# Features of q on both column halves of TensorE: an attention and Fourier-mix kernel, before and after

## The chip, the cores and the metric

The kernel runs on one core of a Trainium2 chip. The metric is the device time of one execution in microseconds (us). The engines are TensorE (PE in the profile, its weight loads PEld), VectorE (DVE), ScalarE (ACT), GpSimd (POOL) and SyncE (SP), which issues the transfers between HBM and on-chip memory.

## What is computed

The inputs q, k, v have 4 batches, 4 heads, 1088 rows and 32 dimensions in float32. S1 and S2 are 8 x 32.

```
phi(x)  = outer product of S1 x and S2 x, 64 features for each row
kv, z   = sum over rows of phi(k) v  and of phi(k)
attn    = (phi(q) kv) / (phi(q) z + 1e-6)            # per head, 32 values a row
x       = the 4 heads beside one another              # 4 x 1088 x 128
u       = x + real(FFT over the 1088 rows and the 128 columns of x)
out     = u + relu(layernorm(u) w_ch1) w_ch2          # w_ch1 128 x 512
```

## The kernel before

One batch at a time is cut into named steps, each on one engine. A text, ORDER, lists all steps of all batches; the kernel emits them in that order, and each engine runs its own in that sequence and waits for what it needs. BANK gives the first of eight PSUM banks for each use, ENGINE the engine where a step can run on several. In the names, the first digit is the batch b.

- **Loads** (ld_q, ld_k, ld_v, ld_w1, ld_w2 on SP, ld_s on ACT). A partition of q holds 34 successive rows: four heads lie on four blocks of 32 partitions. Work on q is done in two windows w of 16 rows and 256 positions a pair; the rows left over are handled by qt_T, qt_f, qt_a, qt_p.
- **Start** (c_... steps, t_... tables of sines, s_t and s_use, which make sa and sb, the operands of S1 and S2, 32 x 64 per head). Dummy matmuls such as 7@0 keep TensorE busy; the number is how many, then the bank.
- **k side**: kT (transposition, L299), kpr (projection, L289), kab (copy from PSUM), kp (products, L76, 16 of them, POOL or DVE), vc and vl (copies of v), kv and kvt (sums over rows, L337), kvz (L343: copies to the operand t_kvz, for each batch two pairs of heads, each head in its own diagonal block of 64 x 33).
- **q side**: qT (L376, transposition of one window, output with a step of 8 elements), qf (qfeat, L383), qa (copy of one factor from PSUM, ACT), qp (L393, product of the two factors, 128 x 1024, DVE). In qfeat, one instruction takes sa or sb of head h (32 rows of the array, 32h on) against 256 columns of qT. Its output goes to 64 partitions of PSUM: heads 0 and 2 to the left column half of the array, heads 1 and 3 to the right. A window takes 4 heads x 2 halves of the columns x 2 factors = 16 instructions.
- **pnd** (L433): products with t_kvz as the moving operand, 66 columns, weights 128 x 64 from qp: two heads on the two partition halves. 32 instructions a batch, and pnt has 4 for the rows left over. Each float32 matmul leaves two records in the trace. Then den and x (L439 to L444: division, result in bf16).
- **Fourier mix and MLP**: fo and eo (folds by symmetry, POOL or DVE), sC and sS (L461, L465), z and zr (copies), mix (L487, L494; it adds x by a matmul with a permutation), and for each mixer g bn (statistics, L515), sd, rc, un (normalization, L532), tr, ut (transposition), ph (L546), rl (relu, L561 on ACT, L563 on DVE), po (L568), fin (copy to the output tile), out (store). There are ten mixers; eight have 512 columns, mixers 4 and 9 have 128.

The order of the work around the change is thus wholly the text ORDER with the banks: a use of a bank waits until the use before it has been read. A group of features takes four banks: q0.0, q0.1 and q1.1 take 0 to 3, q1.0 takes 1 to 4.

Of the kernel before, what the change touches and what calls it, by code (L numbers as in the profile page):

```python
# [52 lines left out]
def program(nc, T, x, bank):  # L53
# [187 lines left out]
    def c_rev(e):  # L241

        nc.gpsimd.memset(T("rev")[:], 0.0)
        nc.gpsimd.affine_select(out=T("rev")[:], in_=T("rev")[:], compare_op=ALU.not_equal, fill=1.0, base=-127,
                                pattern=[[1, 128]], channel_multiplier=1)
    add("c_rev", "POOL", "", "rev", c_rev)
# [126 lines left out]
    def qT(b, w):  # L373

        out = [[1, 8], [-256, 2], [8, 32]] if w == 0 else [[1, 8], [256, 2], [8, 32]]
        nc.vector.transpose(view(T(f"qT{b % 2}"), (256, 512)[w], out), view(T(f"q_in{b}"), (1, 18)[w] * D, [[1, 16 * D]]))  # L376


    def qfeat(b, w):
        for i in range(2):  # L380
            for h in range(H):
                for f, src in enumerate(("sa", "sb")):
                    nc.tensor.matmul(  # L383
                        ps(f"q{b}.{w}", 512 * (2 * (h // 2) + i) + 256 * f, [[1, 256]], 64 * (h % 2), 64),
                        view(T(src), 0, [[1, F]], 32 * h, 32), view(T(f"qT{b % 2}"), 512 * w + 256 * i, [[1, 256]], 32 * h, 32),
                        start=True, stop=True, tile_position=(32 * h, 64 * (h % 2)), skip_group_check=True)
# [36 lines left out]
    def pnd(b, tiles):  # L423

        for s in tiles:
            for pr in range(2):
                for h in range(2):
                    if s < 8:
                        w = s // 2 % 2
                        q = view(T(f"qp{(2 * b + w) % 3}"), 512 * pr + 256 * (s % 2) + 128 * (s // 4 ^ w) + 64 * h, [[1, 64]])  # L430
                    else:
                        q = view(T("qtp"), 256 * pr + 64 * b, [[1, 64]])
                    nc.tensor.matmul(ps(f"nd{b}", 512 * (s // 3) + 132 * (s % 3) + 66 * pr, [[1, 66]], 64 * h, 64), q,  # L433
                                     view(T("kvz"), 2 * KP * b + KP * pr, [[1, 66]]), start=True, stop=True,
                                     tile_position=(0, 64 * h), skip_group_check=True)
# [47 lines left out]
    def mix(b, half):  # L483
        u = f"u{b}.{half}"
        for w in range(2):
            s = (6, 2)[half] if w else 4 * half
            nc.tensor.matmul(ps(u, 256 * w, [[1, 256]]), T("rev" if w else "idb")[:],  # L487
                             view(T(f"x{b}"), 128 * (s + 1 - w), [[256 * w - 128, 2], [1, 128]]),
                             start=(w == 0), stop=False, skip_group_check=True)
# [218 lines left out]
c_wz c_iota ld_q0.0 c_bias c_rows d_turn c_last d_ph d_pm c_kvz c_v12 c_mask c_eye16 t_turn2 c_vt c_v11 ld_s c_v10  # L708
c_idb c_cen t_ph2 c_rev 7@0 s_t qT0.0 s_use 5@1 qf0.0 d_trig t_sin2 t_turn1 ld_k0.0 t_pm2 t_cos2 t_turn0 kT0.0 1@4
kpr0 t_mC qa0.0 ld_k1.0 kab0 ld_v0 kp0.0 qT0.1 kT1.0 kp0.3 kp0.1 kt_pr0 3@6 kpr1 qp0.0 kt_a0 t_ph1 ld_q1.0 qt_T1 qt_T0  # L710
qf0.1 vl0 ld_v1 ld_k2.0 vc0.0 vc0.1 qa0.1 kt_p0 qt_f0 kv0.0 kab1 kvt0 kv0.3 t_ph0 qT1.1 qp0.1 kv0.1 ld_q2.0 ld_w1
ld_v2 ld_v3 ld_q3.1 kt_pr1 ld_k3.1 ld_k3.0 ld_q3.0 kp0.2 ld_w2 kp1.1 kv0.2 t_pm1 qt_a0 vc1.0 kp1.0 kp1.3 kp1.2 qf1.1
vl1 t_pm0 kt_a1 qt_p0 kT2.0 kt_p1 qT1.0 kvz0 t_sin0 qa1.1 t_mS vc1.1 pnd0.0 pnt0 qp1.1 kpr2 pnd0.1 qT2.0 qT2.1 den0 x0
kv1.0 kab2 qf1.0 kv1.2 kv1.1 kvt1 kv1.3 kt_pr2 w1c t_sin1 qa1.0 qp1.0 qt_T2 kt_a2 vl2 kt_p2 kT3.0 kvz1 kp2.1 kp2.2 w1b
t_cos0 kp2.0 qf2.0 fo0.0 fo0.1 vc2.1 kp2.3 eo0.0 qa2.0 vl3 vc2.0 t_cos1 pnd1.0 pnt1 kpr3.0 pnd1.1 qT3.1 kT3.1 kpr3.1
kab3 qt_T3 qp2.0 qf2.1 den1 x1 qa2.1 kv2.2 kv2.3 kv2.1 qt_f1 vc3.1 kvt2 kv2.0 kp3.1 eo0.1 fo1.0 qp2.1 qt_a1 kvz2 qf3.1
vc3.0 kt_pr3 fo1.1 qt_p1 pnd2.0 qa3.1 kt_a3 kt_p3 pnt2 kvt3 eo1.1 t_mP t_mN pnd2.1 qp3.1 sS0 w2b qT3.0 den2 zS0 x2
kp3.0 eo1.0 kp3.3 sC0 kv3.1 sC1 zC1 zC0 mix0 qf3.0 kp3.2 zrC0 fo2.1 fo2.0 eo2.0 bn0 sd0 rc0 un0 zrC1 sS1 qa3.0 zS1
zrS0 kv3.2 kv3.0 kv3.3 tr0 qp3.0 mix2 ut0 ph0.1 kvz3 zrS1 ph0.0 mix1 rl0.1 rl0.0 pnd3.0 pnt3 eo2.1 bn2 sS2 bn1 sd1 rc1
sd2 rc2 pnd3.1 un1 zS2 un2 tr2 ut2 tr1 ut1 po0 den3 x3 fin0 ph1.0 ph1.1 rl1.1 mix3 rl1.0 zrS2 fo3.0 mix4 ph2.1 rl2.1  # L720
ph2.0 po1 sC2 bn3 bn4 fo3.1 eo3.1 rl2.0 po2 sd3 rc3 eo3.0 un3 tr3 sd4 rc4 ut3 zC2 zrC2 sC3 fin1 ph3.1 mix5 un4 fin2
zC3 rl3.1 ph3.0 tr4 bn5 ut4 sd5 rl3.0 sS3 out0 out2 rc5 un5 mix6 zS3 ph4.0 tr5 ut5 bn6 out1 rl4.0 po3 sd6 rc6 un6 fin3
# [3 lines left out]
"""
BANK = dict(w.split("=") for w in """
st=0 w1=6 k0=4 kt0=5 kv0=5 k1=4 kt1=4 kv1=0 k2=4 kt2=5 kv2=7 k3=7 kt3=7 kv3=7 qt0=6 qt1=4 q0.0=0 q0.1=0 nd0=5 z00=2
z10=0 u0.0=2 t0=0 h0.0=6 h0.1=3 u0.1=0 t1=7 h1.0=6 h1.1=3 q1.0=1 q1.1=0 nd1=4 z01=0 z11=0 u1.0=1 t2=6 h2.0=3 h2.1=6
u1.1=2 t3=3 h3.0=6 h3.1=3 u0.2=5 t4=1 h4.0=6 q2.0=0 q2.1=0 nd2=4 z02=6 z12=6 u2.0=0 t5=7 h5.0=6 h5.1=3 u2.1=1 t6=2  # L730
h6.0=3 h6.1=6 q3.0=3 q3.1=0 nd3=3 z03=6 z13=3 u3.0=2 t7=7 h7.0=0 h7.1=3 u3.1=5 t8=3 h8.0=0 h8.1=3 u1.2=6 t9=7 h9.0=7
# [3 lines left out]
d_turn=DVE t_pm2=ACT t_mC=ACT kt_a0=DVE vl0=DVE vc0.0=ACT vc0.1=ACT t_pm1=ACT vl1=ACT t_pm0=ACT kt_a1=DVE t_mS=ACT  # L735
vc1.1=ACT vl2=ACT fo0.0=POOL fo0.1=POOL eo0.0=POOL vl3=ACT vc2.0=ACT vc3.1=ACT eo0.1=POOL fo1.0=POOL kt_a3=DVE w2b=ACT
eo1.0=POOL zC1=DVE fo2.1=POOL fo2.0=POOL eo2.0=POOL zrS0=ACT ut0=DVE zrS1=ACT zS2=DVE un2=ACT rl1.0=DVE fo3.0=POOL
fo3.1=POOL eo3.1=POOL rl2.0=DVE eo3.0=POOL ut3=DVE fin2=DVE ut4=DVE rl4.0=DVE fin4=DVE ut6=DVE fin6=DVE ut7=DVE
ut9=DVE rl7.1=DVE fin9=DVE fin8=DVE
# [32 lines left out]
```

## Time and profile before

| | |
|---|---|
| median of three runs | 91.48 us (90.75 to 91.81) |
| the profiled execution | 91.52 us, its span 89.7 us |
| granted TensorE clock | 0.999 |
| busy: PE, DVE, ACT, POOL | 78.6, 64.2, 56.7, 46.3 us |
| transfers | 9.65 MB, 7.22 MB read |
| a store of 128 KB, of 64 KB, from issue to landing | 2.4 us, 1.7 us |

The span goes from the first to the last instruction; about 1.8 us of the execution lie outside it. A line of a group reads: line, engine, operation, output <- input, shapes, count, then busy time and the mean length of one in ns, then the idle time before it with what ended it. The chain is followed backwards from the last instruction; its pieces are shown in order of time with their start and length.

### The profile page before, as it was taken

The page shows a single profiled execution, that of the slowest core. Times are in us where ns is not written, and L with a number is a line of the kernel's source. Part 1 is how long each engine was busy: PE and PEld are TensorE (multiplying, and loading weights), DVE is VectorE, ACT ScalarE, POOL GpSimd, SP SyncE. Part 2 cuts the span into 40 slices and gives each one's busy share as a digit, 9 for nine tenths or more (in the row PEclk, how much of TensorE's full clock was granted, in tenths as well). Part 3 has the DMA queues.
Part 4 walks back from the last instruction along what each step waited for, and adds up shares of the span by engine and source line. Part 5 has one row for each costly group of instructions (what it writes and reads, how often), then busy time and mean ns, then how long its engine had stood idle before and what let it go on. Part 6 is the DMA issues. An engine that isn't in the chain of part 4 may idle for free.

```text
span 89.7 us, 3227 instructions
## 1 busy us (share of the span) xinstructions
PE 78.6 (88%) x1379; PEld 58.9 (66%) x1385; DVE 64.2 (72%) x130; ACT 56.7 (63%) x101; POOL 46.3 (52%) x73
## 2 busy tenths in 40 slices
PE   4949999899499999999989999998999999889600
PEld 1126688779478589787947787796685777756500
DVE  3879999697884947481998856779866888596300
ACT  2373795649504758482949298856767798899400
POOL 7688099895479980899915950024973020000000
PEclk9999999999999999999999999999999999999999
DMA  2999999993000000000000000000400615007362
GB/s 41 380 359 388 389 421 393 390 358 108 9 7 7 4 0 7 0 11 0 0 7 0 0 0 7 0 0 7 117 0 0 187 54 146 0 0 186 84 167 67
DMA packets 6142, 9.65 MB, mean 108 GB/s; under 512 B 624, under 2 KB 3952, under 8 KB 6128
## 3 DMA queue, kind: packets, MB, share of 16 engines
q1 hardware_dynamic: 6048, 9.44, 31.1%
q8 instruction: 11, 0.18, 0.8%
q14 instruction: 3, 0.02, 0.1%
q10 hardware_dynamic: 80, 0.01, 0.1%
HBM read 7.22 MB, written 2.23 MB: 105 GB/s over the span
## 4 chain that ended last, share of the span: by engine, by line
PE 70%; ACT 8%; DVE 6%; DMA 5%; issue 4%; ACTq 1%; DVEq 0%
PE ps L383 17%; PE ps L337 11%; PE ps L433 8%; PE ps L568 6%; PE ps L546 5%; DMA t_s<-in_S_dram 5%; PE ps L289 4%; PE ps L461 4%; PE ps L494 3%; PE ps L699 2%; ACT t_v_in__96 L561 2%; ACT t_v_in__98 L561 2%; PE ps L487 2%; PE ps L465 2%; PE ps L538 2%
## 5 line engine op out<-in xcount | busy, mean ns | idle before, releaser
L69 ACT COPY t_qa__127<-ps 128x1024 f32<-128x1024 f32 x4 | 4.1, 1013 | 6.7 <-PE ps L383 6.7
L69 ACT COPY t_qa__128<-ps 128x1024 f32<-128x1024 f32 x4 | 4.0, 1012 | 4.8 <-PE ps L383 4.8
L699 PE MATMUL ps<-t_wz 128*128 128x512 bf16 x15 | 5.4, 496 | 1.3 <-DVE t_eps L125 1.2
L383 PE MATMUL ps<-t_qT__114,t_sa 32*64 32x256 f32 x64 | 5.4, 395 | 0.0
L383 PE MATMUL ps<-t_qT__115,t_sa 32*64 32x256 f32 x64 | 5.4, 395 | 0.0
L383 PE MATMUL ps<-t_qT__114,t_sb 32*64 32x256 f32 x64 | 5.2, 374 | 0.0
L383 PE MATMUL ps<-t_qT__115,t_sb 32*64 32x256 f32 x64 | 5.2, 374 | 0.0
L73 POOL COPY t_zr__148<-t_z__144 128x546 bf16<-128x546 bf16 x2 | 1.3, 640 | 7.0 <-DVE t_z__144 L71 6.6
L433 PE MATMUL ps<-t_kvz,t_qp__130 128*64 128x66 f32 x96 | 3.7, 225 | 1.3 <-issue 1.3
L546 PEld LDWEIGHTS <-t_w1b 128*128 128x128 bf16 x40 | 3.2, 97 | 2.4 <-issue 1.2
L433 PEld LDWEIGHTS ps<-t_kvz,t_qp__130 128*64 128x64 f32 x96 | 3.2, 138 | 1.6 <-issue 1.5
L561 ACT ACTIVATE t_v_in__96<-ps 128x1024 bf16<-128x1024 f32 x4 | 3.9, 1020 | 0.4 <-PE ps L494 0.4
L561 ACT ACTIVATE t_v_in__97<-ps 128x1024 bf16<-128x1024 f32 (+1 forms) x4 | 3.6, 920 | 0.7 <-PE ps L546 0.7
L699 PEld LDWEIGHTS <-t_wz 128*128 128x128 bf16 x16 | 1.6, 114 | 3.5 <-issue 1.8
L76 POOL TENSOR_TENSOR t_kp__119<-t_ab__117 128x512 f32<-128x512 f32 x2 | 2.1, 1068 | 2.9 <-ACT t_ab__117 L69 2.9
L383 PEld LDWEIGHTS ps<-t_qT__114,t_sa 32*64 32x64 f32 x64 | 2.3, 130 | 1.9 <-ACT t_kvz L69 0.8
L76 POOL TENSOR_TENSOR t_eo__140<-t_e__138 128x512 bf16<-128x512 bf16 x3 | 3.5, 1152 | 0.1
L76 POOL TENSOR_TENSOR t_eo__141<-t_e__139 128x512 bf16<-128x512 bf16 x3 | 3.4, 1153 | 0.1
L433 PE MATMUL ps<-t_kvz,t_qp__129 128*64 128x66 f32 x96 | 3.4, 224 | 0.0
L433 PEld LDWEIGHTS ps<-t_kvz,t_qp__129 128*64 128x64 f32 x96 | 3.0, 138 | 0.6 <-issue 0.4
L546 PE MATMUL ps<-t_unT__161,t_w1b 128*128 128x512 bf16 (+1 forms) x14 | 3.4, 333 | 0.1
L561 ACT ACTIVATE t_v_in__98<-ps 128x1024 bf16<-128x1024 f32 x3 | 3.0, 1021 | 0.7 <-POOL t_e__139 L76 0.6
(320 smaller groups left out, 267.0 us busy)
## 6 DMA issues: line engine op xcount, KB each, us to landing
out_dram<-t_k_in__93 SPq DMA_DIRECT2D x6, 128.0 KB, 2.4
out_dram<-t_k_in__95 SPq DMA_DIRECT2D x6, 128.0 KB, 2.4
t_q_in__100<-in_q_dram SPq DMA_DIRECT2D x1, 544.0 KB, 3.8
...
t_q_in__101<-in_q_dram SPq DMA_DIRECT2D x1, 544.0 KB, 8.4
...
```

Source lines behind the costliest of these rows:

```text
L69: nc.scalar.copy(out, in_)
L76: (nc.vector if e == "DVE" else nc.gpsimd).tensor_tensor(out=out, in0=in0, in1=in1, op=op)
L289: nc.tensor.matmul(ps(f"k{b}", 64 * t, [[1, 64]], 64 * h, 64), view(T(f"kT{b % 2}"), 64 * (2 * t + h), [[1, 64]]), T("sblk")[:], start=Tru ...
L337: nc.tensor.matmul(ps(f"kv{b}", 33 * (h // 2), [[1, 33]], 64 * (h % 2), 64), w, v, start=(b, h % 2) not in begun, stop=True, tile_position ...
L383: nc.tensor.matmul(ps(f"q{b}.{w}", 512 * (2 * (h // 2) + i) + 256 * f, [[1, 256]], 64 * (h % 2), 64), view(T(src), 0, [[1, F]], 32 * h, 32 ...
L433: nc.tensor.matmul(ps(f"nd{b}", 512 * (s // 3) + 132 * (s % 3) + 66 * pr, [[1, 66]], 64 * h, 64), q, view(T("kvz"), 2 * KP * b + KP * pr, ...
L461: nc.tensor.matmul(ps(f"z{trig}{b}", 512 * c, [[1, NK]]), T(f"eo{b % 2}")[:, trig, c, t, :], T("tab")[:, t, trig, NK * c:NK * c + NK], sta ...
L494: nc.tensor.matmul(ps(u, 256 * w + 128 * t, [[1, 128]]), zcol(b, trig, half, w, t), m, start=False, stop=True, skip_group_check=True)
L546: nc.tensor.matmul(ps(use, 128 * n * i, [[1, 128 * n]]), T("w1b")[:, 128 * c:128 * c + 128], T(f"unT{g % 3}")[:, 0:128 * n], start=True, s ...
L561: nc.scalar.activation(out=out, in_=in_, func=ACT.Relu)
L568: nc.tensor.matmul(ps(u, 128 * t, [[1, 128]]), ht_view(g, 512 * c + 128 * t, [[1, 128]]), T("w2b")[:, c, :], start=False, stop=True, skip_ ...
L699: nc.tensor.matmul(made["ps"][:, at, :], made["wz"][:, 0:128], made["wz"][:], start=True, stop=True)
```

## The change

- **qfeat**: each head is now handled by two instructions per factor that differ in the column half: half v takes the first or the second 16 of each 32 successive columns of qT (one half of the head's rows), both from the same 32 partitions. Their results go to partitions 64v on of one bank per head. The loops run over h, then v, then the factor.
- **qT**: the output of the transposition is contiguous in runs of 32.
- **kvz**: since the two partition halves of the features now belong to one head, each head's block of 64 x 33 is written twice, to both diagonal blocks: four copies a batch for two, the tile and its clearing memset (c_kvz) twice as large.
- **pnd**: 16 blocks (window, tile, head) of two instructions for 8 tiles x 2 pairs x 2; the counts stay the same. The values of x lie in another order, so fold, mix and the row numbers in c_rows follow, and a second permutation (c_fwd) is made for the mix.
- **ORDER, BANK, ENGINE** are all new. The first four groups of features, q0.0, q1.0, q0.1 and q1.1, all take banks 0 to 3. On VectorE instead of GpSimd are kp0.3, kp1.3, kp3.0 and t_turn1; qa3.1 goes from ScalarE to VectorE; many others change too.

```
-        out = [[1, 8], [-256, 2], [8, 32]] if w == 0 else [[1, 8], [256, 2], [8, 32]]
+        out = [[32, 8], [512 * w - 256, 2], [1, 32]]
...
     def qfeat(b, w):
-        for i in range(2):
-            for h in range(H):
+        for h in range(H):
+            for v in range(2):
                 for f, src in enumerate(("sa", "sb")):
                     nc.tensor.matmul(
-                        ps(f"q{b}.{w}", 512 * (2 * (h // 2) + i) + 256 * f, [[1, 256]], 64 * (h % 2), 64),
-                        view(T(src), 0, [[1, F]], 32 * h, 32), view(T(f"qT{b % 2}"), 512 * w + 256 * i, [[1, 256]], 32 * h, 32),
-                        start=True, stop=True, tile_position=(32 * h, 64 * (h % 2)), skip_group_check=True)
+                        ps(f"q{b}.{w}", 512 * h + 256 * f, [[1, 256]], 64 * v, 64), view(T(src), 0, [[1, F]], 32 * h, 32),
+                        view(T(f"qT{b % 2}"), 512 * w + 16 * v, [[256, 2], [32, 8], [1, 16]], 32 * h, 32),
+                        start=True, stop=True, tile_position=(32 * h, 64 * v), skip_group_check=True)
...
     def kvz(b, e):
         for h in range(2):
-            copy(e, view(T("kvz"), 2 * KP * b + 33 * h, [[KP, 2], [1, 33]], 64 * h, 64),
-                 ps(f"kv{b}", 0, [[33, 2], [1, 33]], 64 * h, 64))
+            for v in range(2):
+                copy(e, view(T("kvz"), KP * (H * b + h) + 33 * v, [[2 * KP, 2], [1, 33]], 64 * v, 64),
+                     ps(f"kv{b}", 0, [[33, 2], [1, 33]], 64 * h, 64))
...
+    def pnd(b, blocks):
+        for i in blocks:
+            w, t, hd = i // 8, i // 4 % 2, i % 4
+            for h in range(2):
+                if i < 16:
+                    q = view(T(f"qp{(2 * b + w) % 3}"), 256 * hd + 128 * t + 64 * h, [[1, 64]])
+                    z = view(T("kvz"), KP * (H * b + hd), [[1, 66]])
+                else:
+                    q = view(T("qtp"), 256 * (i - 16) + 64 * b, [[1, 64]])
+                    z = view(T("kvz"), KP * (H * b + 2 * (i - 16)), [[KP + 33, 2], [1, 33]])
+                nc.tensor.matmul(ps(f"nd{b}", 512 * (i // 6) + 66 * (i % 6), [[1, 66]], 64 * h, 64), q, z,
+                                 start=True, stop=True, tile_position=(0, 64 * h), skip_group_check=True)
...
     def fold(b, e, c):
-        tt(e, T(f"e1{b % 2}")[:, c], T(f"x{b}")[:, 0:4, :], T(f"x{b}")[:, 4:8, :], (ALU.add, ALU.subtract)[c])
+        tt(e, T(f"e1{b % 2}")[:, c], view(T(f"x{b}"), 0, [[512 + 32, 2], [64, 8], [1, 32]]),
+           view(T(f"x{b}"), 32, [[512 - 32, 2], [64, 8], [1, 32]]), (ALU.add, ALU.subtract)[c])
...
-    "vt": ([128, 2 * B, VP], FP32), "kvz": ([128, B, 2, KP], FP32),
+    "vt": ([128, 2 * B, VP], FP32), "kvz": ([128, B, H, KP], FP32),
```

The new ORDER, with stretches of it left out:

```
c_wz c_iota ld_q0.0 c_bias c_rows c_eye16 c_mask c_idb t_turn1 ld_s c_last ld_k1.0 ld_k0.0 c_fwd c_rev c_vt c_cen 7@0
s_t t_turn0 c_kvz t_ph1 t_turn2 c_v11 t_pm1 t_cos1 qT0.0 qt_T0 s_use 3@1 qf0.0 qT0.1 kT1.0 ld_q1.0 qa0.0 t_ph0 t_pm0
kT0.0 ld_v0 4@4 kpr1 kab1 t_sin0 t_sin1 kp1.0 t_cos0 c_v12 c_v10 vc0.1 qt_T1 2@5 kpr0 ld_w1 qt_f0 kab0 kp0.2 ld_v1 vl1
kt_pr0 kt_pr1 qp0.0 qT1.0 kp0.1 ld_k2.0 qt_a0 kt_a0 qt_p0 kp0.0 qf1.0 vc1.0 kp0.3 kt_p0 vl0 kt_a1 t_ph2 vc0.0 qa1.0
w1c w1b t_pm2 vc1.1 kv0.3 kvt0 kv0.2 qp1.0 ld_k3.0 ld_k3.1 ld_q3.0 ld_q2.0 ld_w2 ld_v3 kv0.1 qf0.1 kv0.0 t_mP kT2.0
kp1.3 qT1.1 kpr2 kp1.1 kt_p1 kv1.3 kvt1 kv1.0 qa0.1 qp0.1 kab2 t_sin2 ld_v2 ld_q3.1 kv1.1 kvz0 qf1.1 pnd0.0 t_mS qa1.1
kp1.2 kv1.2 kT3.1 pnd0.1 pnt0 qT2.0 qT2.1 kT3.0 kvz1 kp2.3 qp1.1 kt_pr2 t_cos2 kt_a2 vc2.0 vc2.1 vl2 pnt1 qt_T2 den0
kt_p2 x0 qt_T3 pnd1.1 pnd1.0 qf2.1 den1 kpr3.0 kpr3.1 x1 qa2.1 qp2.1 kvt2 kp2.1 kv2.1 qt_f1 fo0.1 kp2.2 kp2.0 vc3.1
...
kv3.2 den2 x2 fo2.1 kt_pr3 zC1 d_ph qf3.1 zC0 kt_a3 d_pm d_trig kt_p3 qa3.1 qp3.1 sS1 zS1 kvt3 kv3.1 mix0 kvz3 mix2
bn0 bn2 sd0 rc0 un0 zrS1 sd2 pnd3.0 zrC1 fo2.0 eo2.0 eo2.1 pnt3 sC2 zrS0 zrC0 pnd3.1 zC2 rc2 tr0 ut0 sS2 zS2 mix1
...
out6 out5 tr8 out7 ut8 mix4 bn4 mix9 rl3.0 rl3.1 sd4 ph8.1 ph8.0 bn9 rc4 rl8.1 po3 sd9 un4 tr4 rl8.0 po8 fin8 fin3 rc9
out3 ut4 un9 out8 tr9 ph4.0 ut9 ph9.0 rl4.0 po4 fin4 out4 rl9.0 po9 fin9 out9
```

and the old one's end:

```
ph9.0 ph7.0 rl9.0 po8 po9 fin9 out9 fin8 out8 rl7.0 po7 fin7 out7
```

More of the change, by code (lines that the diff above doesn't have):

```diff
@@ L239, in program, with order @@
     add("c_idb", "POOL", "", "idb", lambda e: eye(T("idb")[:], 128))
[L241 to L246, printed above, removed]
+    def order(n, sign, base):
+        t = T(n)[:]
+        nc.gpsimd.memset(t, 0.0)
+        nc.gpsimd.affine_select(out=t, in_=t, compare_op=ALU.not_equal, fill=1.0, base=base,
+                                pattern=[[sign, 16], [16 * sign, 8]], channel_multiplier=1)
+    add("c_fwd", "POOL", "", "fwd", lambda e: order("fwd", -1, 0))
+    add("c_rev", "POOL", "", "rev", lambda e: order("rev", 1, -127))
     def c_mask(e):
@@ L421, in program @@
         add(f"qt_p{i}", "DVE", f"pqt:{i} qta:{i}", f"qtp:{i}", lambda e, i=i: qt_p(i), f"qt{i}:2")
[L423 to L435, printed above, removed]
+    def pnd(b, blocks):
[10 more added lines that the diff above has]
+                                 start=True, stop=True, tile_position=(0, 64 * h), skip_group_check=True)
     def den(b):
@@ L485, in mix @@
         for w in range(2):
-            s = (6, 2)[half] if w else 4 * half
-            nc.tensor.matmul(ps(u, 256 * w, [[1, 256]]), T("rev" if w else "idb")[:],
-                             view(T(f"x{b}"), 128 * (s + 1 - w), [[256 * w - 128, 2], [1, 128]]),
+            nc.tensor.matmul(ps(u, 256 * w, [[1, 256]]), T("rev" if w else "fwd")[:],
+                             view(T(f"x{b}"), 512 * w + 256 * (1 - w) + 32 * half, [[512 * w - 256, 2], [64, 4], [1, 32]]),
                              start=(w == 0), stop=False, skip_group_check=True)
@@ L621, in program @@
             add(f"pnd{b}.{pr}", "PE", f"qp:{2 * b + pr} kvz:{b}", f"pnd:{b}/{pr}",
-                lambda e, b=b, pr=pr: pnd(b, [4 * v + 2 * pr + t for v in range(2) for t in range(2)]), f"nd{b}:3")
-        add(f"pnt{b}", "PE", f"qtp:{b // 2} kvz:{b}", f"pnd:{b}/2", lambda e, b=b: pnd(b, (8,)), f"nd{b}:3")
+                lambda e, b=b, pr=pr: pnd(b, range(8 * pr, 8 * pr + 8)), f"nd{b}:3")
+        add(f"pnt{b}", "PE", f"qtp:{b // 2} kvz:{b}", f"pnd:{b}/2", lambda e, b=b: pnd(b, (16, 17)), f"nd{b}:3")
         add(f"den{b}", "DVE", f"pnd:{b}", f"den:{b}", lambda e, b=b: den(b), f"nd{b}:3")
@@ L634, in program @@
         for half in range(2):
-            mixer(b, half, g, (f"zC:{b} zS:{b}", f"zrC:{b} zrS:{b}")[half] + f" x:{b} idb rev cd sd")
+            mixer(b, half, g, (f"zC:{b} zS:{b}", f"zrC:{b} zrS:{b}")[half] + f" x:{b} fwd rev cd sd")
             g += 1
@@ L707 @@
 ORDER = """
[L708 to L722, printed above, removed]
@@ new lines @@
+kt_p2 x0 qt_T3 pnd1.1 pnd1.0 qf2.1 den1 kpr3.0 kpr3.1 x1 qa2.1 qp2.1 kvt2 kp2.1 kv2.1 qt_f1 fo0.1 kp2.2 kp2.0 vc3.1
+vc3.0 fo0.0 fo1.0 qf2.0 kv2.0 kv2.2 kv2.3 qT3.1 t_mN t_mC w2b qT3.0 kab3 qt_a1 qa2.0 qt_p1 eo0.1 sS0 kp3.3 fo1.1 vl3
+qp2.0 kp3.2 eo0.0 eo1.1 kp3.1 d_turn kvz2 kv3.3 zS0 qf3.0 eo1.0 kp3.0 pnd2.1 qa3.0 pnt2 pnd2.0 kv3.0 qp3.0 sC1 sC0
+kv3.2 den2 x2 fo2.1 kt_pr3 zC1 d_ph qf3.1 zC0 kt_a3 d_pm d_trig kt_p3 qa3.1 qp3.1 sS1 zS1 kvt3 kv3.1 mix0 kvz3 mix2
+bn0 bn2 sd0 rc0 un0 zrS1 sd2 pnd3.0 zrC1 fo2.0 eo2.0 eo2.1 pnt3 sC2 zrS0 zrC0 pnd3.1 zC2 rc2 tr0 ut0 sS2 zS2 mix1
@@ new lines @@
+ph0.1 un2 rl0.1 den3 x3 fo3.1 bn1 tr2 ut2 ph0.0 rl0.0 sd1 fo3.0 rc1 eo3.0 mix5 ph2.1 rl2.1 ph2.0 rl2.0 po0 sC3 fin0
+eo3.1 sS3 un1 bn5 zC3 zrS2 tr1 ut1 zS3 sd5 po2 ph1.1 rl1.1 zrC2 ph1.0 rc5 fin2 un5 rl1.0 mix6 bn6 sd6 mix7 zrS3 zrC3
+bn7 tr5 rc6 un6 ut5 sd7 po1 fin1 ph5.0 rc7 rl5.0 un7 tr6 ph5.1 ut6 ph6.0 out0 out2 rl5.1 out1 rl6.0 mix3 bn3 ph6.1
+rl6.1 tr7 ut7 po5 ph7.1 fin5 sd3 rl7.1 ph7.0 po6 rl7.0 rc3 un3 fin6 mix8 bn8 tr3 po7 ut3 sd8 rc8 un8 fin7 ph3.0 ph3.1
+out6 out5 tr8 out7 ut8 mix4 bn4 mix9 rl3.0 rl3.1 sd4 ph8.1 ph8.0 bn9 rc4 rl8.1 po3 sd9 un4 tr4 rl8.0 po8 fin8 fin3 rc9
@@ L726 @@
+out3 ut4 un9 out8 tr9 ph4.0 ut9 ph9.0 rl4.0 po4 fin4 out4 rl9.0 po9 fin9 out9
 """
 BANK = dict(w.split("=") for w in """
[L728 to L731, printed above, removed]
+st=0 w1=6 k0=5 kt0=4 kv0=4 k1=4 kt1=5 kv1=7 k2=6 kt2=7 kv2=0 k3=7 kt3=0 kv3=7 qt0=6 qt1=1 q0.0=0 q0.1=0 nd0=4 z00=5
@@ L732 @@
+z10=1 u0.0=0 t0=4 h0.0=2 h0.1=6 u0.1=4 t1=0 h1.0=2 h1.1=6 q1.0=0 q1.1=0 nd1=0 z01=3 z11=5 u1.0=5 t2=1 h2.0=2 h2.1=6
+u1.1=2 t3=0 h3.0=3 h3.1=6 u0.2=5 t4=3 h4.0=2 q2.0=3 q2.1=3 nd2=0 z02=6 z12=6 u2.0=1 t5=6 h5.0=6 h5.1=3 u2.1=0 t6=2
+h6.0=6 h6.1=3 q3.0=3 q3.1=1 nd3=1 z03=6 z13=2 u3.0=5 t7=6 h7.0=3 h7.1=6 u3.1=1 t8=0 h8.0=6 h8.1=3 u1.2=0 t9=3 h9.0=3
 """.split())
@@ L734 @@
 ENGINE = dict(w.split("=") for w in """
[L735 to L739, printed above, removed]
+t_turn1=DVE t_pm1=ACT t_pm0=ACT qt_a0=DVE kt_a0=DVE kp0.3=DVE vl0=ACT kt_a1=DVE vc0.0=ACT t_pm2=ACT vc1.1=ACT
+kp1.3=DVE t_mS=ACT vc2.0=ACT vc2.1=ACT vl2=ACT fo0.0=POOL fo1.0=POOL t_mC=ACT w2b=ACT eo0.1=POOL fo1.1=POOL eo0.0=POOL
+eo1.1=POOL kp3.0=DVE kt_a3=DVE qa3.1=DVE zrS1=ACT fo2.0=POOL eo2.0=POOL eo2.1=POOL fo3.1=POOL ut2=DVE rl0.0=DVE
+fo3.0=POOL rl2.0=DVE eo3.1=POOL ut1=DVE zrC2=DVE fin2=DVE ut6=DVE rl5.1=DVE rl6.1=DVE rl7.1=DVE ut3=DVE fin7=DVE
+ut8=DVE rl8.1=DVE un4=ACT fin3=DVE ut4=DVE ut9=DVE rl9.0=DVE
 """.split())
```

11 lines of the change are left out of this document (4 added, 7 removed).

## The prediction

> **What bounds the kernel now.** I read the page first (spans of the engines, then the chain), then the engines' busy time in stretches, then the timeline of one group of feature matmuls, and the chain in order of time.
>
> ```profile
> span 89.7 us, 3227 instructions
> PE 78.6 (88%) x1379; PEld 58.9 (66%) x1385; DVE 64.2 (72%) x130; ACT 56.7 (63%) x101; POOL 46.3 (52%) x73
> ...
> PE 70%; ACT 8%; DVE 6%; DMA 5%; issue 4%; ACTq 1%; DVEq 0%
> PE ps L383 17%; PE ps L337 11%; PE ps L433 8%; PE ps L568 6%; PE ps L546 5%; DMA t_s<-in_S_dram 5%; PE ps L289 4%; PE ps L461 4%; PE ps L494 3%; PE ps L699 2%; ACT t_v_in__96 L561 2%; ACT t_v_in__98 L561 2%; PE ps L487 2%; PE ps L465 2%; PE ps L538 2%
> ```
>
> TensorE is the longest engine, 70% of the chain is its work, and the largest item is line 383, the features of q: 17% of 89.7 is 15.6 us. The stretches (columns: length, busy time of PE, PEld, DVE, ACT, POOL, granted clock, DMA share and GB/s) show where that holds:
>
> ```profile
> 5.57:12.40 6.83, 6.53 (x113) 4.42 (x115) 6.83 (x11) 4.69 (x9) 4.26 (x11) 1.00 1.01 391
> 12.40:42.40 30.00, 28.32 (x662) 23.17 (x662) 21.76 (x33) 17.46 (x36) 23.57 (x25) 1.00 0.32 111
> 42.40:54.70 12.30, 11.94 (x230) 9.27 (x230) 9.65 (x16) 8.92 (x14) 7.48 (x8) 1.00 0.01 3
> 54.70:84.50 29.80, 28.59 (x378) 21.14 (x381) 22.60 (x52) 22.99 (x39) 7.09 (x8) 1.00 0.21 57
> 84.50:89.70 5.20, 0.02 (x1) 0.00 (x0) 0.00 (x0) 0.58 (x1) 0.00 (x0) 0.99 0.42 114
> ```
>
> Up to 54.7 us, where the second mixer's sum has been formed, TensorE is busy for 40.3 of 42.3 us, GpSimd for 31.1, VectorE for 31.4, ScalarE for 26.4. So time taken from TensorE there shortens the span until another engine is full, and the nearest has 9 us to spare. The clock is 1.00 throughout. The profiled execution took 91.52 us, 1.82 more than its span; the median of the runs is 91.48, so no correction is needed.
>
> **The features of q.** Chain in order of time (start, length), and the timeline of the group at 12.34:
>
> ```profile
> 7.10 1.99 PE ps L383 x32
> ...
> 12.41 1.95 PE ps L383 x32
> ...
> 34.03 0.94 PE ps L433 x32
> ```
> ```profile
> 12.34 0.68 PE L383 MATMUL ps<-t_qT__114,t_sa 32*64 32x256 f32 x8
> 12.82 0.63 PE L383 MATMUL ps<-t_qT__114,t_sb 32*64 32x256 f32 x8
> 13.25 0.67 PE L383 MATMUL ps<-t_qT__114,t_sa 32*64 32x256 f32 x8
> 13.69 0.67 PE L383 MATMUL ps<-t_qT__114,t_sb 32*64 32x256 f32 x8
> ```
>
> One group is 16 instructions; each leaves two records, 32 in all. The code issues sa, sb, sa, sb, head by head, yet the trace has eight records of sa, then eight of sb: the four heads run side by side, each on its own 32 rows, and each row block works off its own list. From 13.25 to 13.69 two records per row block pass, so one 256-column record takes 0.22 us. Eight in a row per row block are 1.75 us, and with start-up 1.95. At any moment four tiles of 32x64 work, and half of the array's columns beside them are idle: even heads use the left half, odd heads the right.
>
> The change gives each head both halves: eight tiles, four records deep. That is 4 x 0.22 = 0.87, plus about 0.18 for the first weights and the later starts of eight tiles: 1.05 us. It holds if two column halves of the same rows stream at once. The evidence is line 433: 32 records of 66 columns in 0.94 us, 29 ns each. Line 383 needs 0.22 / 256 = 0.86 ns per column, so 66 columns are 57 ns: two at a time, one on each half, over all 128 rows. Bounds per group: 0.87 (perfect) to 1.95 (the halves take turns); I take 1.05, being nearest the row that shows both halves at work. Eight groups, all on the chain: 8 x (1.95 - 1.05) = **-7.2 us**.
>
> The weight loads of the same group (PEld):
>
> ```profile
> 12.61 0.39 PEld L383 LDWEIGHTS ps<-t_qT__114,t_sb 32*64 32x64 f32 x8
> ```
>
> [...]
>
> **The other parts.** Durations (groups by line; mean ns of one after the bar's first number):
>
> ```profile
> L376 DVE STREAM_TRANSPOSE t_qT__115<-t_q_in__101 128x512 f32<-128x512 f32 x2 | 2.2, 1106 | 0.0
> L299 DVE STREAM_TRANSPOSE t_kT__109<-t_k_in__93 128x512 f32<-128x512 f32 x1 | 0.7, 691 | 0.0
> L393 DVE TENSOR_TENSOR t_qp__131<-ps,t_qa__127 128x1024 f32<-128x1024 f32 x1 | 1.2, 1224 | 1.5 <-ACT t_qa__127 L69 1.5
> L563 DVE TENSOR_SCALAR t_v_in__97<-ps 128x1024 bf16<-128x1024 f32 x1 | 1.2, 1225 | 0.1
> L515 DVE BATCH_NORM_STATS2 t_st__150<-ps 128x6 f32<-128x256 f32 x5 | 1.9, 422 | 0.2 <-PE ps L494 0.2
> L532 DVE TENSOR_TENSOR t_un__158<-ps,t_sm__157 128x512 bf16<-128x512 f32 x1 | 0.7, 692 | 0.0
> L444 DVE TENSOR_TENSOR t_x__137<-ps,t_den__133 128x1152 bf16<-128x1152 f32 x1 | 1.4, 1357 | 0.0
> L71 DVE COPY t_k_in__95<-ps 128x512 f32<-128x512 f32 x2 | 1.4, 682 | 0.0
> L71 DVE COPY t_unT__161<-ps 128x512 bf16<-128x512 bf16 x3 | 1.3, 424 | 1.4 <-PE ps L538 1.4
> L523 DVE RECIPROCAL t_sm__155<-t_sm__155 128x4 f32<-128x4 f32 x2 | 0.4, 178 | 0.7 <-ACT t_sm__155 L518 0.7
> ```
> ```profile
> L69 ACT COPY t_qa__127<-ps 128x1024 f32<-128x1024 f32 x4 | 4.1, 1013 | 6.7 <-PE ps L383 6.7
> L69 ACT COPY t_kvz<-ps 64x66 f32<-64x66 f32 x8 | 1.7, 209 | 1.5 <-PE ps L337 1.3
> L76 POOL TENSOR_TENSOR t_kp__119<-t_ab__117 128x512 f32<-128x512 f32 x2 | 2.1, 1068 | 2.9 <-ACT t_ab__117 L69 2.9
> L261 POOL MEMSET t_kvz<- 128x544 f32 x1 | 0.6, 555 | 0.0
> L244 POOL TENSOR_SCALAR_AFFINE_SELECT t_rev<-t_rev 128x128 bf16<-128x128 bf16 x1 | 0.3, 292 | 0.1
> ```
>
> Transposition of q, 8 times: today 1.10 us with an output step of 8; the keys' of the same size with a step of 2 takes 0.69. Contiguous I take 0.69, bounds 0.5 and 1.10: 3.3 us less on VectorE. It shortens the path only at the start, where s_use stands behind the first transposition on VectorE: features can begin about 1.10 - 0.69 earlier than 7.10, **-0.4**. Elsewhere it is room, spent next.
>
> kp0.3, kp1.3, kp3.0 and t_turn1 go to VectorE. A product of 512 there: 0.65, near half of line 393's 1.22 (bounds 0.6, that half, and 1.07, GpSimd's own). Three take 1.9 us there and free 3.2 on GpSimd; t_turn1 adds under 1. qa3.1 moves to VectorE too (1.2, like line 563).
>
> k-v's operand: four copies for two, 4 x 2 x 0.209 = +1.7 us on ScalarE. pnd waits for all four. In the new order qf1.1 stands before pnd0.0 and covers them; for kvz1 nothing long does, and pnt1, pnd1 and the next qf2.1 queue behind: up to 0.4 us each, in the give-back below. The clearing memset doubles, +0.56, and the new permutation costs about 0.5, both on GpSimd before its first product, where it waits 2.1 to 2.9 us today; uncovered they cost 1.06.
>
> pnd, fold and mix have the same instruction counts (72 records per batch in pnd; operands of fold and mix in runs of 32 elements): zero; if such runs slowed fold by a tenth, it would be hidden on GpSimd in the middle of the kernel. SP: the same loads; v0 comes fifth instead of fourth, w1 ahead of v1 and k2. A load of 544 KB passes in about 1.4 us at the 391 GB/s of the stretch from 5.57, so v0 is there by 11; kv0 begins only about 14.
>
> **The new order.** Its end is shorter. Today the last work is a full mixer's:
>
> ```profile
> 79.75 1.95 ACT t_v_in__96 L561 x2
> ...
> 84.56 0.58 ACT t_k_in__94 L69
> ```
>
> In the new order mixers 4 and 9, a quarter as large, come last: the final fin copies 128 columns for 512 and one store of 64 KB goes out for two of 128. Against 1.95 + 0.58 and 5.2 us of drain I take **-1.0** (bounds 0 and -2.5).
>
> Given back: the other engines get tighter. After mix2 VectorE still has, in the new order, 18 statistics (7.6), 8 normalizations (5.5), 6 relus (7.4), x3 with its denominators (1.9), 5 transposed copies (2.1), 3 fins (2.0), 10 reciprocals (1.7) and the small mixers' (1.4): 29.6 us, against 28.6 of TensorE in that stretch today and 22.6 of VectorE. TensorE arrives at mix2 earlier than the 7.2 explains, because this work was put behind it, but two equally long engines that wait on each other don't both run without gaps. I take **+1.5** for this and the kvz waits, near the bound of 0 (everything overlaps), since neither engine's list alone is longer than today's 29.8 us. The other bound is 7: with VectorE idle there for today's 24% the stretch is 29.6 / 0.76 = 39 us, 9 longer than today, of which the 2.0 us that TensorE idles before 54.7 may come back.
>
> Sum: -7.2 - 0.4 - 1.0 + 1.5 = -7.1; 91.5 - 7.1 = **84.4 us**.
>
> **Rivals.**
> (a) The other engines take the gain: VectorE in the last 35 us, or the chain feature, qa, qp (1.05 + 1.01 + 1.22 and four banks held throughout), since the first four groups share banks 0 to 3. The give-back is then 7: 89.9 us. For it: VectorE's 29.6. Against: ScalarE waited 6.7 us for line 383 in one group of rows alone, so TensorE was the late one.
> (b) It goes better: the start moves further and the waits of today's order vanish; give-back 0 and the end -2.5: 81.4.
> (c) The two halves of the same rows take turns. The group stays at 1.95: 84.4 + 7.2 = 91.6, no change. Only line 433's rate is against it, and its two halves read the same kvz, where here they read different columns of qT.
> (d) Slower: the list that a row block works off takes no second tile while the first is pending, and hand-out stops. Loads of weights in 13.03:13.25, and then in 13.25:13.46:
>
> ```profile
> 13.04 0.13 PEld L383 LDWEIGHTS ps<-t_qT__114,t_sa 32*64 32x64 f32 x1
> ```
> ```profile
> 13.26 0.21 PEld L383 LDWEIGHTS ps<-t_qT__114,t_sa 32*64 32x64 f32 x7
> ```
>
> At the second half of a group only the first head's load comes early; the other heads' come 0.2 us later, once the first head's matmul has started: hand-out stood still behind a row block with a full list. The new code puts a head's 16 entries in one row block before the next head's. If the list is per row block and not per tile, the next head starts after about five of eight records: 3 x 5 x 0.22 + 8 x 0.22 = 5.0 us a group, 84.4 + 8 x 3.95 = 116 us. It decides against the change from 1.95 us a group on. Against it: in line 433 both halves, which share all rows, start together. [...]
>
> **How the numbers follow.** 84.4 has 0.62, its own range 81.5 to 87; (a) 0.15; (b) 0.10; (c) 0.07; (d) 0.06. A range of 80.5 to 90 holds the first three, bar edges, and leaves out (c) and (d). A measurement here tells about 1% from no change. Faster: 0.62 + 0.15 + 0.10 and a little of (c): 0.88; the rest of (c), 0.05, the same; (d) and a bad order, 0.07, slower.
>
> **What would show it.** Right: the features' line at about 1.05 us a group, eight times on the chain or off it, with sa records sixteen at a time; transposition of q near 0.69; mix2 near 45; the last stores of 64 KB. Wrong: a group at 1.95 or 5; VectorE idle before statistics late in the span (rival a); TensorE waiting on t_kvz for over 0.4 us a time.

## The result and the profile after

The changed kernel takes 85.78 us (median of four runs, 85.23 to 86.87); the one before, run beside it, 91.65 (90.75 to 91.81). The ratio is 0.936, with a 95% interval of 0.925 to 0.946. The forecast was 84.4 us, range 80.5 to 90.0. All ratios here compare undisturbed runs alone, and a median, which takes in the slow ones, can lie up to 1.4 us above what its ratio gives; the granted clock of TensorE was lower in some of those (a mean of 0.942 in one of 88.54 us) and hardly in others (0.993 in one of 87.12 us).

The page of the changed kernel (span, busy time of the engines, shares of the chain):

```profile
span 83.6 us, 3240 instructions
PE 72.5 (87%) x1380; PEld 53.6 (64%) x1385; DVE 67.7 (81%) x136; ACT 54.0 (65%) x101; POOL 46.0 (55%) x75
...
PE 63%; DVE 12%; DMA 8%; issue 6%; ACT 5%; ACTq 1%; DVEq 0%
```

TensorE is busy 6.1 us less, the very difference of the spans (89.7 - 83.6); the profiled execution took 85.36 us. VectorE's part of the chain has doubled to 12%. The same stretches as in the forecast, cut at the start of the work, at 12.4 us, at the end of the second mixer's sum, and at the last matmul (columns as there):

```profile
5.24:12.40 7.16, 7.00 (x148) 4.77 (x157) 6.52 (x14) 5.78 (x12) 5.47 (x12) 1.00 1.03 401
12.40:47.77 35.37, 32.88 (x855) 26.57 (x838) 30.29 (x45) 23.68 (x51) 30.97 (x35) 1.00 0.27 93
47.77:79.10 31.33, 29.47 (x383) 21.39 (x386) 27.33 (x59) 22.18 (x37) 5.53 (x6) 1.00 0.21 56
79.10:83.60 4.50, 0.00 (x0) 0.00 (x0) 0.00 (x0) 0.27 (x1) 0.00 (x0) 0.92 0.42 117
```

The second mixer's sum is complete at 47.77 us instead of 54.70: that stretch alone gives 6.9 us. The next is 1.5 us longer than before (31.33 for 29.8), and the drain 0.7 shorter (4.5 for 5.2). 6.9 - 1.5 + 0.7 = 6.1.

The timeline of one group of features, matmuls and then weight loads:

```profile
36.29 0.73 PE L387 MATMUL ps<-t_qT__116,t_sa 32*64 32x256 f32 x16
36.78 0.68 PE L387 MATMUL ps<-t_qT__116,t_sb 32*64 32x256 f32 x16
```
```profile
36.56 0.44 PEld L387 LDWEIGHTS ps<-t_qT__116,t_sb 32*64 32x64 f32 x16
```

There are sixteen records of sa, then sixteen of sb, where the code issues sa, sb, sa, sb: all eight tiles work side by side, each through its own two instructions. And the weights of sb are loaded from 36.56 to 37.00, while sa's matmuls run on the same rows (to 37.02). The chain in order of time shows what a group costs, and the main holes:

```profile
6.20 1.10 PE ps L387 x32
...
11.96 1.09 PE ps L387 x32
...
20.32 1.49 issue
...
22.47 1.10 PE ps L387 x32
...
42.74 1.16 DVE t_ph L175
43.91 0.08 DVE t_kta__112 L71
43.99 0.07 DVE t_pm L183
44.06 0.93 issue
44.99 0.29 DVE t_ktp__114 L311
...
75.80 0.69 DVE t_k_in__94 L71
76.52 3.15 DMA out_dram<-t_k_in__94
79.76 0.27 ACT t_k_in__94 L69
```

A group takes 1.10 us for 1.95. Seven of the eight stand in the chain. The eighth (42.38 to 43.54) runs while VectorE holds the chain, and TensorE waits for 0.98 us behind it. At 20.32 TensorE stands still for 1.49 us without any wait that the profile shows (the kernel before has such a hole too, 1.33 us at 22.38). At 44 it waits for VectorE, which is at d_ph and d_pm (lines 175 and 183). At the end a store stands in the chain: the last output tile shares its buffer with an earlier store.

### The profile page after: what moved, and what is told of

Read it like the earlier page. It is cut to its first block, busy times and chain, and to the rows that moved or that the text cites. A ratio compares the mean times of both kernels' runs of the same rounds, so it can differ in the third digit from the quotient of the medians.

```text
span 83.6 us, 3240 instructions
## 1 busy us (share of the span) xinstructions
PE 72.5 (87%) x1380; PEld 53.6 (64%) x1385; DVE 67.7 (81%) x136; ACT 54.0 (65%) x101; POOL 46.0 (55%) x75
## 4 chain that ended last, share of the span: by engine, by line
PE 63%; DVE 12%; DMA 8%; issue 6%; ACT 5%; ACTq 1%; DVEq 0%
PE ps L339 11%; PE ps L387 9%; PE ps L439 8%; PE ps L573 6%; PE ps L291 5%; PE ps L551 5%; DMA t_s<-in_S_dram 4%; DMA out_dram<-t_k_in__94 4%; PE ps L499 3%; PE ps L467 3%; PE ps L704 3%; PE ps L492 2%; PE ps L543 2%; DVE t_x__137 L449 2%; PE ps L409 1%
## 5 line engine op out<-in xcount | busy, mean ns | idle before, releaser
L69 ACT COPY t_qa__128<-ps 128x1024 f32<-128x1024 f32 x4 | 4.0, 1012 | 2.5 <-PE ps L387 2.5
L69 ACT COPY t_qa__129<-ps 128x1024 f32<-128x1024 f32 x3 | 3.0, 1013 | 3.3 <-PE ps L387 2.9
L69 ACT COPY t_kvz<-ps 64x66 f32<-64x66 f32 x16 | 3.3, 209 | 1.1 <-PE ps L339 0.9
L566 ACT ACTIVATE t_v_in__100<-ps 128x1024 bf16<-128x1024 f32 x3 | 3.0, 1022 | 1.0 <-PE ps L573 0.9
L566 ACT ACTIVATE t_v_in__98<-ps 128x1024 bf16<-128x1024 f32 x3 | 3.0, 1022 | 0.7 <-PE ps L573 0.7
L551 PE MATMUL ps<-t_unT__164,t_w1b 128*128 128x512 bf16 x12 | 3.4, 379 | 0.0
L397 DVE TENSOR_TENSOR t_qp__130<-ps,t_qa__129 128x1024 f32<-128x1024 f32 x1 | 1.2, 1225 | 2.5 <-ACT t_qa__129 L69 2.5
L397 DVE TENSOR_TENSOR t_qp__130<-ps,t_qa__128 128x1024 f32<-128x1024 f32 x2 | 2.4, 1205 | 0.9 <-ACT t_qa__128 L69 0.9
L566 ACT ACTIVATE t_v_in__97<-ps 128x1024 bf16<-128x1024 f32 (+1 forms) x3 | 2.6, 881 | 0.7 <-PE ps L499 0.7
L387 PE MATMUL ps<-t_qT__115,t_sa 32*64 32x256 f32 x64 | 3.1, 399 | 0.0
L69 ACT CAST t_z__144<-ps 128x546 bf16<-128x546 f32 x2 | 1.5, 769 | 2.3 <-PE ps L471 2.3
L566 ACT ACTIVATE t_v_in__99<-ps 128x1024 bf16<-128x1024 f32 x2 | 2.0, 1024 | 1.5 <-PE ps L551 1.5
```

Source lines behind the costliest of these rows:

```text
L69: nc.scalar.copy(out, in_)
L387: nc.tensor.matmul(ps(f"q{b}.{w}", 512 * h + 256 * f, [[1, 256]], 64 * v, 64), view(T(src), 0, [[1, F]], 32 * h, 32), view(T(f"qT{b % 2}") ...
L397: nc.vector.tensor_tensor(out=view(T(f"qp{(2 * b + w) % 3}"), 127 * w, [[256, 4], [128, 2], [1 - 2 * w, 128]]), in0=ps(f"q{b}.{w}", 256, [ ...
L551: nc.tensor.matmul(ps(use, 128 * n * i, [[1, 128 * n]]), T("w1b")[:, 128 * c:128 * c + 128], T(f"unT{g % 3}")[:, 0:128 * n], start=True, s ...
L566: nc.scalar.activation(out=out, in_=in_, func=ACT.Relu)
```

## The experiments

**Code or order?** Two kernels part the change: the new code with the ORDER, BANK and ENGINE of before (plus the step c_fwd, which it needs), and the old code with the new ones (less c_fwd).

```
 e1: new functions      + old ORDER, BANK, ENGINE (c_fwd added before c_rev)
 e2: functions of before + new ORDER, BANK, ENGINE (c_fwd left out)
```

> The changed code with the old texts for order, banks and engines (the new permutation is made just before the old one). Theory (TensorE's work on q's features is on the path, so the code alone brings the gain): eight groups at 1.1 instead of 1.95 us, less what two more operand copies a batch cost; 85.5 to 87.5 us, and 1.1 us a group in the trace. Rival (the new order brings the gain and the features were covered in the old one): 90 to 92 us, with TensorE idle where the groups shrank.

> The old code with the new order, banks and engines. Theory: the groups stay at 1.95 us and on the path, the order alone gains nothing or loses: 91 to 94 us. Rival (the order brings the gain): 85.5 to 87.5 us.

The code alone takes 86.62 us, ratio 0.945 (0.939 to 0.952); the order alone 90.64 us, 0.979 (0.970 to 0.988), where I had expected it to gain nothing. The chain of the code alone, then of the order alone:

```profile
11.45 1.09 PE ps L387 x32
...
20.54 2.46 issue
```
```profile
14.89 1.95 PE ps L383 x32
```

The length of a group goes with the code, whatever the order. The two parts multiply to 0.945 x 0.979 = 0.925; together they give 0.936 (0.925 to 0.946), so on top of the code the order is worth some 1%, less than these intervals can separate. Without the new order the doubled copies of k-v's operand are on the path: in the chain of the code alone they hold 1.8% of 84.8 us, and in the changed kernel TensorE waits for no copy.

**The features alone in the new order.** Loops and views of qfeat go back, all else stays changed.

```
-        for h in range(H):
-            for v in range(2):
+        for i in range(2):
+            for h in range(H):
...
-        view(T(f"qT{b % 2}"), 512 * w + 16 * v, [[256, 2], [32, 8], [1, 16]], 32 * h, 32), ... tile_position=(32 * h, 64 * v)
+        view(T(f"qT{b % 2}"), 512 * w + 256 * i, [[1, 256]], 32 * h, 32), ... tile_position=(32 * h, 64 * (h % 2))
```

> The changed kernel with the old loop of features alone: heads on alternate column halves, eight records deep per row block. The features of the rows are then paired with the wrong operands; only its time is read. Theory: 8 x 0.85 = 6.8 us back on TensorE, of which most shows: 91 to 93 us. Rival (VectorE sets the time of the new order, TensorE has room): under 88 us.

It takes 90.84 us, ratio 0.981 (0.972 to 0.990). Its groups:

```profile
14.98 1.95 PE ps L387 x32
```

With one column half for each head the group is back at 1.95 us and some 4 us of the gain (0.981 against 0.936) are gone. The layout of q, k-v's operand and the order, all kept here, don't give it by themselves: it takes the two column halves.

**Is the contiguous transposition only room on VectorE?** Here qT is written as before with a step of 8, and the features read it with that step.

```
-        out = [[32, 8], [512 * w - 256, 2], [1, 32]]
+        out = [[1, 8], [512 * w - 256, 2], [8, 32]]
...
-        512 * w + 16 * v, [[256, 2], [32, 8], [1, 16]]
+        512 * w + 128 * v, [[256, 2], [1, 8], [8, 16]]
```

> The changed kernel with the transposition of q writing with a step of 8 again, and the features reading qT with that step. Theory: transposition 1.1 instead of 0.69 us, 3.3 us more on VectorE, which now is 81% busy; 0.4 at the start and about half of the rest on the path: 87 to 88.5 us; the groups stay at 1.1 us, since a float32 matmul takes its columns at 0.86 ns each. Rival 1 (VectorE's time is covered): 85.8 us. Rival 2 (reading with a step slows the matmuls): groups well over 1.1 us and over 89 us.

It takes 90.95 us, ratio 0.989 (0.982 to 0.996): nearly the whole gain is gone. The chain, and the groups by line:

```profile
5.12 0.20 PE ps L269
...
6.07 2.06 PE ps L387 x32
...
12.79 2.05 PE ps L387 x32
```
```profile
L387 PE MATMUL ps<-t_qT__115,t_sa 32*64 32x256 f32 x64 | 4.9, 641 | 0.0
...
L380 DVE STREAM_TRANSPOSE t_qT__116<-t_q_in__102 128x512 f32<-128x512 f32 x2 | 2.2, 1102 | 0.0
```

VectorE's transposition is 1.10 us again, as forecast, but what decides is the row above: a record of the features takes 641 ns on average, where the changed kernel has 399. Both halves still work side by side (one half alone with this step takes 3.84 us a group, as the next experiment shows), each at about half its rate. I had called the contiguous transposition room on VectorE; it is the condition of the gain. Before the change the step of 8 stood in what VectorE wrote, so that each head's half was contiguous for TensorE.

**Which step costs what?** One kernel gives each of its eight groups another step in reading qT and either both halves for each head or, as before, one.

```
+        dims = {0: [[1, 256]], 2: [[2, 256]], 4: [[1, 2], [4, 128]], 8: [[1, 4], [8, 64]]}
+        step, both = {(0, 0): (0, 1), (1, 0): (2, 1), (0, 1): (4, 1), (1, 1): (8, 1),
+                      (2, 1): (0, 0), (2, 0): (2, 0), (3, 0): (4, 0), (3, 1): (8, 0)}[b, w]
```

> The changed kernel with another reading pattern of qT in each of the eight groups of features: both column halves with a step of 1, 2, 4 and 8 elements (in the order of the text q0.0, q1.0, q0.1, q1.1), then heads on alternate halves with 1, 2, 4 and 8 (q2.1, q2.0, q3.0, q3.1). The features are of wrong columns; only the length of the groups is read. Theory A (two halves double what is read from the same partitions, and a step wastes that reading): both halves 1.1 us at step 1, growing with the step to about 2.05 at 8; alternate halves 1.95 at every step. Theory B (a step slows any float32 matmul): alternate halves at step 8 take near 3.7 us.

The chain, group by group; from the first to the eighth they are: both halves with steps 1, 2, 4, 8, then one half with steps 1, 2, 4, 8:

```profile
7.05 1.99 PE ps L391 x32
...
13.70 1.14 PE ps L391 x32
...
17.99 2.02 PE ps L391 x32
...
23.59 2.06 PE ps L391 x32
...
30.59 1.95 PE ps L391 x32
...
35.18 1.91 PE ps L391 x32
...
40.00 3.77 PE ps L391 x32
...
48.76 3.84 PE ps L391 x32
```

The first group can't be used, because TensorE is slow there even before it: the three dummy matmuls just before it hold 1.39 us of the chain, where in the changed kernel they hold 0.75, though the granted clock is shown as 1.00 over the group (6.98 to 9.00 us). From 9.03 us on four of them pass in 0.97, as in the changed kernel. The other groups are plain: a step of 2 elements costs nothing (1.14 us for the changed kernel's 1.10, and 1.91 for 1.95), steps of 4 and 8 double the time (2.02 and 2.06; 3.77 and 3.84), whether one or both column halves read. So the doubling doesn't need two halves that read at once: it comes with one alone (1.91 to 3.77), and it sets in between steps of 2 and 4 elements, which are 8 and 16 bytes of float32. What sets it there, no run here shows.

**Does the order inside a group matter?** The loop over halves outside that over heads, so that successive instructions lie on different rows.

```
-        for h in range(H):
-            for v in range(2):
+        for v in range(2):
+            for h in range(H):
```

> The changed kernel with the loop over column halves outside the loop over heads. If a list of pending instructions belongs to each tile, the order within the group is indifferent: 1.10 us a group. If the row block has one list, the changed kernel's order would have stalled and this one would be faster; since the group there took 1.10, no more than 0.05 is expected here.

There is one run, 84.61 us beside 91.41 for the kernel before, with groups of 1.09 to 1.25 us, as in the changed kernel (36.36 1.25 there is the longest of the chain). The hand-out is not held by a pending tile on the same rows, which was rival (d)'s mechanism.

**The two holes that the new order left.** d_turn, d_ph and d_pm move ahead to batch 2; the last output tile gets a buffer of its own; both; and, against the suspicion that the four copies of k-v's operand cost something, a kernel with only two copies a batch.

```
 e7:  kT3.0 kvz1             ->  kT3.0 d_turn d_ph d_pm kvz1   (taken out of their later places)
 e8:  T(f"k_in{g % 3}")      ->  T("ot9" if g == 9 else f"k_in{g % 3}")
 e9:  both
 e10: for v in range(2):     ->  for v in (h,):                (in kvz)
```

> The changed kernel with the small table's steps d_turn, d_ph, d_pm moved from the middle, where GpSimd works beside them and they took 1.2 and 1.1 us, to 22 us, where VectorE waits 2.5 us for a copy. Theory (VectorE holds TensorE up at 44 us through kt_p3): d_ph and d_pm at 0.35 and 0.43 us, TensorE's wait of 1.0 us for t_ktp gone, 84.3 to 85.0 us. Rival (what comes after the second mixer's sum sets the end by itself): 85.6 to 86.

> The changed kernel with an output tile of its own for the last mixer, so that its last copy does not wait for the store of mixer 3. Theory: the wait of 0.8 us goes, 85.0 to 85.4 us. Rival (the stores stand in one queue, which sets the end anyway): 85.6 to 85.9.

> Both of these together. Theory: the gains add, 83.5 to 84.4 us. Rival: as with the better one alone.

> The changed kernel without the second set of copies of k-v's operand (two copies a batch, not four; half of the operand stays zero and the output is wrong, only the time is read). Theory (the copies cost up to 0.4 us a batch on the way to pnd): 84.8 to 85.3 us. Rival (covered by other work of TensorE): 85.6 to 85.9.

Ratios to the kernel before: 0.925 (0.919 to 0.930), 0.943 (0.937 to 0.948), 0.924 (0.918 to 0.930), 0.943 (0.938 to 0.947), medians 85.34, 86.91, 86.14 and 87.34 us. The unaltered kernel (0.936 above) was not run beside these four. Against it the own tile gains nothing, nor does taking two copies out, and the own tile adds nothing to the earlier steps. That store and those copies stood in a chain, or beside it, without setting the end: with its own tile the kernel ends 4.3 us after the last matmul, for 4.5. The earlier d_ph and d_pm look like a gain: the wait at 44 us is gone, and on this chip the two kernels that have them lie below the two that don't, with intervals that don't meet. VectorE's and GpSimd's timelines in the first of them show what went on beside the steps when they were short:

```profile
22.64 0.31 DVE L175 SCALAR_TENSOR_TENSOR t_ph<-t_dd,t_sr,t_ph 128x128 f32<-128x128 f32 x1
22.99 0.23 DVE L183 TENSOR_SCALAR t_pm<-t_ph 128x128 int32<-128x128 int32 x1
```
```profile
23.34 1.06 POOL L76 TENSOR_TENSOR t_kp__124<-t_ab__117 128x512 f32<-128x512 f32 x1 [1.83 <-PE ps L339]
```

Here GpSimd had waited 1.83 us and began only when both were done. In the changed kernel the same two run beside GpSimd's folds (42.43 to 43.76, and two more from 43.84 on) and take four to five times as long:

```profile
42.67 1.24 DVE L175 SCALAR_TENSOR_TENSOR t_ph<-t_dd,t_sr,t_ph 128x128 f32<-128x128 f32 x1
...
43.94 1.14 DVE L183 TENSOR_SCALAR t_pm<-t_ph 128x128 int32<-128x128 int32 x1
```
```profile
42.43 1.33 POOL L76 TENSOR_TENSOR t_e__139<-t_x__137 128x512 bf16<-128x512 bf16 x1
```

Through what the two engines hold each other up, no run here shows. To have the unaltered changed kernel for comparison, I ran it beside the earlier d_ph and d_pm on one more chip.

> The changed kernel unaltered, as the measure for the next run on the same chip: 85.2 to 86.5 us, 0.93 to 0.945 of the kernel before.

> The changed kernel with d_turn, d_ph and d_pm moved to 22 us, beside the unaltered one. Theory (the hold-up of TensorE by t_ktp at 44 us was on the path): 0.7 to 1.2 us below it. Rival (TensorE arrives earlier at the second mixer's sum and waits there for VectorE): within 0.3 us of it.

Medians 86.14 (85.05 to 88.67) and 85.83 us (84.44 to 87.5); the changed kernel's ratio is 0.931 (0.925 to 0.937), for the other these runs gave none. That ratio overlaps the 0.925 (0.919 to 0.930) of the earlier steps, so the times don't show a gain. In the second of these kernels the steps came beside GpSimd by half, which the timelines show:

```profile
24.06 0.31 DVE L175 SCALAR_TENSOR_TENSOR t_ph<-t_dd,t_sr,t_ph 128x128 f32<-128x128 f32 x1
24.40 1.13 DVE L183 TENSOR_SCALAR t_pm<-t_ph 128x128 int32<-128x128 int32 x1
```
```profile
24.39 1.06 POOL L76 TENSOR_TENSOR t_kp__124<-t_ab__117 128x512 f32<-128x512 f32 x1 [1.45 <-PE ps L339]
```

GpSimd began at 24.39, between the two: the first took 0.31 us, the second 1.13. The traces say more than the times. From the start of the first group to the end of the last matmul the changed order takes 72.9 us in each of three traces (two of the changed kernel, one with the loops exchanged), and with the earlier steps 72.0; in the other two traces with them it takes 72.3 and 72.5, although the first group was 0.7 and 0.9 us longer there. So the earlier steps save some 0.9 us on TensorE's path, even where d_pm is slow. How much of that reaches the end of the execution stays open: the medians of the last pair differ by 0.3 us, the ratios of the four kernels (0.943 against 0.925) by 1.7. No kernel here beats the changed one beyond doubt by its time.

## Why the prediction was right, step by step

- **The features: right, the forecast a little large.** Forecast 8 x (1.95 - 1.05) = 7.2, measured 8 x (1.95 - 1.10) = 6.8 us in the profile; putting the old features back in the new order costs some 4 us of time. The working held as well: eight tiles side by side, each with four records. That all eight groups lie on the chain did not hold: the eighth doesn't, and its 0.85 us end in a wait (see the give-back). Weights loaded beside running matmuls on the same rows: sb's from 36.56 to 37.00, with sa's matmuls until 37.02, and in the kernel before, with one tile a row block, from 12.61 to 13.00, with sa's until 13.02. Rivals (c) and (d) fall by that timeline and the 1.10 us a group.
- **The transposition: size right, role wrong.** 0.69 forecast, 0.67 to 0.71 measured. The groups of it by tile:

```profile
L380 DVE STREAM_TRANSPOSE t_qT__115<-t_q_in__101 128x512 f32<-128x512 f32 x2 | 1.4, 706 | 0.1
...
L380 DVE STREAM_TRANSPOSE t_qT__115<-t_q_in__103 128x512 f32<-128x512 f32 x2 | 1.3, 668 | 0.0
```

  But the step "Elsewhere it is room" missed that the feature term hangs on it: reading with a step of 8 takes 2.05 us a group. The 7.2 came out near because the change has both, the halves and the layout; each alone gives little (0.981 and 0.989). That part was luck.
- **The start.** Forecast -0.4; the first group begins at 6.20 for 7.10, -0.9. Of this 0.46 is the transfer of S, whose transposition on TensorE (line 269, 267 before) begins at 5.24 instead of 5.71. That is chance: the transfer took between 3.62 and 5.88 us in the executions with the new order. The other 0.44 has the size that was forecast, but not the cause. From the transposition of S to the first group pass 0.96 us in the changed kernel (1.39 before), and 0.95 in the kernel that writes qT with a step of 8 (5.12 to 6.07 above), whose transposition takes 1.10 us as before; with the short transposition in the old order the chain runs through that (5.90 to 6.52), and the first group begins at 6.94. In the new order VectorE begins to transpose q at 4.42, before S has landed, instead of at 5.61. So the order moved the start, and the size was met by luck.
- **The end.** Forecast -1.0, drain measured 0.7 shorter. It fits the mechanism named, a quarter-sized mixer last; the term was 0.3 too large.
- **The give-back.** Forecast 1.5, measured 0.8 + 1.5 = 2.3 us; this is the mis-sized term. 54.7 - 6.8 - 0.9 would put the second mixer's sum at 47.0; it came at 47.77. Those 0.8 are not the k-v operand's copies, as I had it: TensorE waits for none of them, and the kernel with half as many is no faster. They go with the wait of 0.98 us at 44, where the products of keys left over stand on VectorE behind d_ph and d_pm. With these two moved away that wait is gone, the eighth group stands in the chain, and the second mixer's sum comes 40.7 us after the start of the first group (6.67 to 47.38) for 41.6 in the changed kernel. I had not costed that d_ph and d_pm were moved to where GpSimd works. The products of 512 that went to VectorE:

```profile
L76 DVE TENSOR_TENSOR t_kp__119<-t_ab__118 128x512 f32<-128x512 f32 x1 | 1.5, 1548 | 0.0
...
L76 DVE TENSOR_TENSOR t_kp__120<-t_ab__118 128x512 f32<-128x512 f32 x1 | 1.0, 958 | 0.0
L76 DVE TENSOR_TENSOR t_kp__122<-t_ab__117 128x512 f32<-128x512 f32 x1 | 0.7, 692 | 0.0
```

  I took 0.65 with bounds of 0.6 and 1.07; only the shortest comes near, and the longest, which began 0.24 us after a product on GpSimd, is beyond the bound: GpSimd's own duration was no upper bound where both work at once. After the mixer's sum the stretch grew by 1.5 us, as rival (a) would have it but far from its 7: VectorE is busy for 27.3 of 31.3 us (I had listed 29.6), and TensorE for 29.5. "Near 45" for the second mixer was therefore wrong: the order put only 0.9 us of TensorE's work behind it (29.47 for 28.59).
- **What was expected to be covered.** The clearing memset takes 1.005 us for 0.555 and the sixteen copies 3.3 us for 1.7; neither stands in the chain.

The sum in the profile is -6.8 - 0.9 + 0.8 + 1.5 - 0.7 = -6.1 us for a forecast of -7.1. The give-back was 0.8 worse than forecast, the features 0.4 and the end 0.3; the start, by chance and by the order, was 0.5 better.
